# An FNet block with a GEGLU feed-forward: the DFT stage's side work laid out by a planner in the kernel

## The chip, the cores and the metric

One core of a Trainium2 chip. The metric is the device time of one execution in microseconds: the median of several runs of the kernel.

## What is computed

x has 2048 rows (the sequence) of 448 features, in f32. The weights of the two DFTs are given as matrices.

```python
a = einsum("bsd,ed->bse", ln(x), dft_hid_re)       # the hidden DFT, real and imaginary part
b = einsum("bsd,ed->bse", ln(x), dft_hid_im)
h = x + einsum("ts,bse->bte", dft_seq_re, a) - einsum("ts,bse->bte", dft_seq_im, b)
g = einsum("bsd,df->bsf", ln(h), w_gate)           # df = 1792
u = einsum("bsd,df->bsf", ln(h), w_up)
out = h + einsum("bsf,fd->bsd", gelu(g) * u, w_down)
```

ln is a layer norm without weights, gelu the tanh form.

## The kernel before, in words

Every f32 operand is split into two f16 halves, a high one (ACT rounds, `hi_part`, L105) and a low one (DVE subtracts the high half from the source, `lo_part`, L109 and L111), and each product is three matmuls: high by high, high by low, low by high. TensorE (PE) has by far the most work; ACT and DVE make its operands.

**The hidden DFT.** 16 tiles of 128 rows of x are normalised, split, turned by DMA transposes and multiplied (`feature_mm`, L422): a "feature tile", 22 matmuls of 448 columns, slot `F` in the code. `feature_out` takes the result out of PSUM. Half of the tiles (units 0 to 3) are split at once. The others (units 4 to 7) are kept in f32 in `b32`, a tile of the pool `ring` with tag "w" and two buffers; POOL (GpSimd) forms Strassen sums of them (`feature_sums`, L460 to L462) and `feature_split` splits these.

**The sequence DFT.** The 2048 x 2048 matrices are used in 8 passes `p` (256 rows of the result each, in four PSUM banks `acc`) of 8 units `u` (256 of the 2048 inputs). A unit's weights are loaded as f32 (`wr`, 512 KB, four buffers, L475). For a plain unit (0 to 3) they are split into `ws`, and PE does 24 matmuls of 448 columns (L518). For a Strassen unit (4 to 7) DVE first forms four sums (`wsum`, L480 to L482, two buffers); seven blocks are split into `ws` (three buffers), and PE does 42 matmuls of 224 columns. At the end of a pass `seq_out` adds the banks into `hx`, the residual stream, which is stored; its moments are taken, and for the first four passes (tokens of quarters 0 and 1) it is normalised, summed, split and transposed into `hops`, the moving operand of the gate and up products.

**The side work.** Gate and up weights come as 14 sets of f32 (`gu_raw`). Each needs four sums (L581 to L587, DVE) and four splits in pieces of 4, 2, 4 and 4 blocks, which gives a tile of 896 KB that is stored to `w_dram` (L626) and read back once per quarter (`gw`, L845). Ten sets are made during the DFTs, in a tile `gu_w` that also lies in `ring`, tag "w": one finished set can stand where `b32` wants to go. Sets 0, 1 and 2 come last and stay in SBUF for the first quarter. The other four sets (4, 7, 10, 13) are made in the first quarter in six "beats" each.

**The order.** PE's slots are a list: feature tiles, with units of pass 0 between them, then passes 1 to 7. Everything else is given to the slot numbers by hand: `plan(n, rank, what)` puts an action into slot `n`, and the slots are then written out in turn, sorted by rank. Each engine runs its own instructions in the order written and waits where an operand isn't there.

**The gate and up products.** 56 steps `t`, four quarters of 14. A step has 39 matmuls of 256 columns (L970) in seven products: `x_open` 6, `z_open` 6, `y_open` 6, `x_close` 5, `y_mid` 6, `y_close` 5, `z_close` 5. Between them ACT copies a bank (pY, L1009), takes u2 and u3 out of the bank Y (L1014, L1028) and does the gelu (g1, L1023; c12, L1047); DVE makes the hidden values hh. In the first quarter the down weights are prepared beside it by `down_prep`, a set for two steps: POOL makes sums `wd_s` (L215 to L218), ACT and DVE split the raw part (`down_hi(n, 0)`, `down_lo(n, 0)`) and the sums (`down_hi(n, 1)`, `down_lo(n, 1)`). From step 14 on the down products (L913) run between the gate and up products.

Of the kernel before, what the change touches and what calls it, by code (L numbers as in the profile page):

```python
# [32 lines left out]
def kernel(  # L33
# [262 lines left out]
    S_UNITS, WR = (4, 5, 6, 7), 3  # L296
# [142 lines left out]
    def feature_out(i):  # L439
        ps = feat.pop(i)  # L440
        if not is_s(i // 2):
            t = bop[i] = dft.tile([P, 2, 4, HD], F16, name=f"b{i}")
            for r in range(2):
                src, sc = ps[r][:, :D], (SC_AB, -SC_AB)[r]
                hi_part(t[:, 0, 2 * r : 2 * r + 2].rearrange("p o d -> p (o d)"), src, sc)
                lo_part(
                    t[:, 1, 2 * r : 2 * r + 2].rearrange("p o d -> p (o d)"),
                    src,
                    t[:, 0, 2 * r : 2 * r + 2].rearrange("p o d -> p (o d)"),
                    sc,  # L450
                )
            return
        b = b32[i] = ring.tile([P, 8, HD], F32, tag="w", bufs=2, name=f"b32_{i}")
        for r in range(2):
            hi_part(b[:, 2 * r : 2 * r + 2].rearrange("p o d -> p (o d)"), ps[r][:, :D], (SC_AB, -SC_AB)[r])


# [6 lines left out]
    def feature_split(i):  # L464
        b = b32.pop(i)
        t = bop[i] = dft.tile([P, 2, 7, HD], F16, name=f"b{i}")
        hi_part(t[:, 0], b[:, 1:8])
        lo_part(t[:, 1], b[:, 1:8], t[:, 0])
# [15 lines left out]
    def seq_split(p, u):  # L484
        r = wr.pop((p, u))
        t = ws[p, u] = dft.tile([P, 2, 7, 2 * P], F16, tag="ws", bufs=3, name=f"ws{p}_{u}")
        parts = [(slice(0, 1), r[:, 0:1]), (slice(1, 3), r[:, 2:4]), (slice(3, 7), wsum.pop((p, u)))] if is_s(u) else [(slice(0, 4), r)]
        for dst, src in parts:
            hi_part(t[:, 0, dst], src, D_SC)
        for dst, src in parts:  # L490
            lo_part(t[:, 1, dst], src, t[:, 0, dst], D_SC)

# [15 lines left out]
    def seq_mm(p, u, first, last):  # L508
# [4 lines left out]
        for cc in range(2):  # L513
# [7 lines left out]
            if is_s(u):  # L521
                for a, o, k, half in PRODUCTS:
                    for m, (lb, lw) in enumerate(TERMS):
                        mm(k, slice(half * HD, half * HD + HD), w[:, lw, a, cc * P : (cc + 1) * P], b[:, lb, o], end and m == 2)
            else:
                for k, a0 in ((0, 0), (1, 1)):
                    for r in range(2):
                        for m, (lb, lw) in enumerate(TERMS):
                            rhs = b[:, lb, 2 * r : 2 * r + 2].rearrange("p o d -> p (o d)")
                            mm(k, slice(0, D), w[:, lw, a0 + 2 * r, cc * P : (cc + 1) * P], rhs, end and r == 1 and m == 2)  # L530
# [12 lines left out]

    def seq_out(p):
        (X, Y, Z, W), _ = acc.pop(p)
        h = hp[divmod(p, 2)]
        e = e_of[p] = fops.tile([P, 4, HD], F32, tag="tt", name=f"e{p}")
        stt = V.scalar_tensor_tensor
        A.activation(e[:, 1], Z[:, 0:HD], AF.Copy, scale=SC_Y)
# [18 lines left out]
    class Weights:  # L568


        def __init__(self, f, pool, w_of):
            self.f, self.pool, self.w_of = f, pool, w_of
# [29 lines left out]

        def beat(self, k):

            if k < 2:
                self.sums(k == 0, k == 1)
            if k == 1:
                self.w = self.w_of()
            parts = self.parts(True) + self.parts(False)
# [6 lines left out]

        def split(self, of_raw):
            if of_raw:
                self.w = self.w_of()
            for s0, s1, src in self.parts(of_raw):  # L620
                hi_part(self.slots(0, s0, s1, src), src, W_SC)
            for s0, s1, src in self.parts(of_raw):
                lo_part(self.slots(1, s0, s1, src), src, self.slots(0, s0, s1, src), W_SC)
# [33 lines left out]

    for k, (i, i2) in enumerate(tiles_of):
# [728 lines left out]
```

## Time and profile before

| | before |
|---|---|
| median of 3 runs | 729.01 us (728.94 to 729.23) |
| the profiled execution | 729.15 us |
| its span | 727.4 us |
| PE busy | 708.2 us, 97% |
| DVE busy | 529.1 us, 73% |
| ACT busy | 396.1 us, 54% |
| POOL busy | 215.3 us, 30% |
| first gate/up matmul | at 361.58 us |

An engine's queue is run in order, so an instruction that waits holds all behind it. In a timeline row stand start, length, engine, line, operation, the tiles written and read, the shape and the count; the brackets give the idle time of the engine before it and what ended it. In a list of waits a row reads "engine tile line waited for engine tile line: us in total, times, the longest". In the table of windows each engine has its busy time and its count of instructions; granted clock, DMA share and GB/s stand at the end.

### The profile page before, as it was taken

The numbers are of one execution on the slowest core, as the hardware profiler recorded it, in microseconds if no ns is written. First come the engines' busy times: TensorE is split into PE (matmuls) and PEld (weight loads), VectorE is DVE, ScalarE is ACT, GpSimd is POOL, SyncE is SP. The second block draws the span as 40 slices with busy tenths as digits, with TensorE's granted clock in tenths as the row PEclk, the third lists the DMA queues.
The fourth block names the chain that finished last, engine by engine and source line by source line (L and its number), as shares of the span: only waits on it lengthen the run. The fifth ranks groups of instructions, "written<-read, shape, count | busy, mean of one in ns | idle before, by whom it ended". The sixth has DMA issues, their size and how long they took to land.

```text
span 727.4 us, 14930 instructions
## 1 busy us (share of the span) xinstructions
PE 708.2 (97%) x5944; PEld 574.1 (79%) x5944; DVE 529.1 (73%) x1054; ACT 396.1 (54%) x836; POOL 215.3 (30%) x241
## 2 busy tenths in 40 slices
PE   7999997989999999999998899999999999999998
PEld 5556555767777777686887789999999999999998
DVE  6777859698989998988478887576665756667520
ACT  5575646465757664645266665456555545555510
POOL 0023150000000000010025574465563756657230
PEclk9999999999999999999999999999999999999999
DMA  8464444656889697774268564957459486655401
GB/s 326 114 132 100 112 154 132 242 142 216 214 294 239 235 273 269 248 242 158 95 249 293 210 226 168 198 179 220 164 172 197 167 215 224 205 199 203 153 14 64
DMA packets 71765, 139.24 MB, mean 191 GB/s; under 512 B 41232, under 2 KB 47504, under 8 KB 71696
## 3 DMA queue, kind: packets, MB, share of 16 engines
q1 hardware_dynamic: 71696, 138.30, 60.8%
q8 instruction: 46, 0.75, 0.5%
q14 instruction: 23, 0.19, 0.1%
HBM read 108.79 MB, written 20.19 MB: 177 GB/s over the span
## 4 chain that ended last, share of the span: by engine, by line
PE 73%; DVE 13%; ACT 8%; issue 3%; DMA 2%; POOL 1%; SPq 0%; ACTq 0%; DVEq 0%
PE acc L518 29%; PE pY L970 13%; PE acc_d L913 11%; PE pX L970 8%; PE pZ L970 8%; DVE ws L111 2%; ACT ws L105 2%; ACT b L105 1%; DVE xs L109 1%; DVE st_x L328 1%; PE last_Z L1132 1%; PE last_X L1132 1%; PE last_Y L1132 1%; DVE b L109 1%; ACT x L355 1%
## 5 line engine op out<-in xcount | busy, mean ns | idle before, releaser
L518 PE MATMUL acc<-b,ws 128*128 128x224 f16 (+1 forms) x2112 | 277.4, 293 | 6.0 <-DVE ws L111 5.4
L518 PEld LDWEIGHTS <-ws 128*128 128x128 f16 x2112 | 202.8, 98 | 80.2 <-DVE ws L111 9.5
L970 PEld LDWEIGHTS <-gw 128*128 128x128 f16 x2067 | 201.9, 98 | 27.8 <-issue 7.3
L970 PE MATMUL pY<-hops,gw 128*128 128x256 f16 x901 | 122.5, 273 | 5.1 <-ACT pY L1009 5.1
L913 PE MATMUL acc_d<-wd,dn_w 128*128 128x224 f16 x882 | 105.1, 259 | 0.0
L111 DVE SCALAR_TENSOR_TENSOR ws<-wr,ws 128x256 f16<-128x256 f32 (+2 forms) x96 | 73.4, 790 | 19.3 <-ACT ws L105 18.7
L913 PEld LDWEIGHTS <-dn_w 128*128 128x128 f16 x882 | 85.0, 98 | 2.8
L105 ACT ACTIVATE ws<-wr 128x256 f16<-128x256 f32 (+2 forms) x96 | 63.0, 690 | 39.9 <-PE acc L518 21.5
L970 PE MATMUL pZ<-hops,gw 128*128 128x256 f16 x583 | 81.0, 273 | 0.8 <-DVE hh L980 0.7
L970 PE MATMUL pX<-hops,gw 128*128 128x256 f16 x583 | 79.2, 273 | 0.0
L1049 POOL TENSOR_TENSOR hh<-hh,c 128x256 f32<-128x256 f32 x42 | 32.1, 764 | 146.1 <-ACT c L1047 146.1
L215 POOL TENSOR_TENSOR wd_s<-wd 128x448 f32<-128x448 f32 x7 | 8.8, 1254 | 215.9 <-DVE wsum L480 199.3
L422 PEld LDWEIGHTS <-xT 128*128 128x128 f16 x352 | 34.2, 98 | 32.3 <-issue 1.2
L109 DVE TENSOR_TENSOR dn_w<-hh,dn_w 128x256 f16<-128x256 f32 x42 | 19.6, 467 | 53.1 <-ACT dn_w L105 53.1
L1063 POOL TENSOR_TENSOR dn_s<-hh 128x256 f32<-128x256 f32 x42 | 52.8, 1258 | 0.0
L105 ACT ACTIVATE ws<-wsum 128x1024 f16<-128x1024 f32 x32 | 33.6, 1050 | 35.1 <-DVE wsum L482 35.0
L109 DVE TENSOR_TENSOR dn_w<-dn_s,dn_w 128x640 f16<-128x640 f32 x42 | 46.3, 1103 | 6.2 <-ACT dn_w L105 4.4
L1014 ACT ACTIVATE u<-pY 128x256 f32<-128x256 f32 x56 | 21.5, 383 | 52.2 <-PE pY L970 52.1
L1009 ACT ACTIVATE pY<-pX 128x256 f32<-128x256 f32 x56 | 20.7, 369 | 49.1 <-PE pX L970 49.1
L422 PE MATMUL ab<-wh_hi,xT 128*128 128x448 f16 x224 | 45.5, 352 | 0.3 <-DVE b L111 0.2
L111 DVE SCALAR_TENSOR_TENSOR ws<-wsum,ws 128x1024 f16<-128x1024 f32 x32 | 39.1, 1222 | 2.6 <-ACT ws L105 2.6
L1062 POOL TENSOR_TENSOR dn_s<-hh 128x256 f32<-128x256 f32 x42 | 38.5, 916 | 0.0
(137 smaller groups left out, 937.0 us busy)
## 6 DMA issues: line engine op xcount, KB each, us to landing
gw<-w_dram SPq DMA_DIRECT2D x49, 896.0 KB, 4.8
wr<-in_w_seq_dram SPq DMA_DIRECT2D x64, 512.0 KB, 4.4
gu_raw<-in_w_gu_dram SPq DMA_DIRECT2D x28, 384.0 KB, 4.9
w_dram<-gu_w SPq DMA_DIRECT2D x10, 896.0 KB, 6.8
wd<-in_w_down_dram SPq DMA_DIRECT2D x14, 448.0 KB, 4.9
hx<-in_x_dram SPq DMA_DIRECT2D x8, 448.0 KB, 6.6
h_dram<-hx SPq DMA_DIRECT2D x8, 448.0 KB, 5.7
w_dram<-gw SPq DMA_DIRECT2D x4, 896.0 KB, 5.9
```

Source lines behind the costliest of these rows:

```text
L105: A.activation(dst, src, AF.Copy, scale=scale)
L109: V.tensor_sub(dst, src, hi)
L111: V.scalar_tensor_tensor(dst, src, scale, hi, op0=ALU.mult, op1=ALU.subtract)
L422: PE.matmul(feat[i][r][:, :D], xT[i][:, kx, :], w[:, kw, r * D : (r + 1) * D], start=n == 0, stop=n == 10,)
L518: PE.matmul(banks[k][:, cols], lhs, rhs, start=k not in begun, stop=stop, skip_group_check=True)
L913: PE.matmul(acc[k // 2][:, k % 2 * HD : (k % 2 + 1) * HD], a_of(la, a), b_of(lb, b), start=first and m == 0 and k % 2 == 0, stop=last and ...
L970: PE.matmul(ps, w[:, wl, wa + ws, :], ops[:, m + ms, :], start=first and n == 0, stop=last and n == len(terms) - 1, skip_group_check=True,)
L1014: A.activation(self.u2, self.Y, AF.Copy, scale=SC)
L1049: G.tensor_mul(c22, c22, self.c12)
L1062: G.tensor_add(s[:, 0:2], t[:, 0:2], t[:, 2:4])
L1063: G.tensor_sub(s[:, 2:4], t[:, 1:4:2], t[:, 0:4:2])
L1132: PE.matmul(banks[0][:, c * HD : (c + 1) * HD] if one else banks[c][:, 0:HD], last["h"][:, lh, f, tok], w, start=f == 0 and m == 0 and c = ...
```

## The change

1. **The planner.** All actions of the DFT stage from slot 3 on become `Task`s with an engine, a duration, a due time and the tasks that they follow (`lag` is a latency after these). Slots of PE are tasks too, with the lengths 4.16, 4.54 and 4.02 us. `arranged()` runs a clock in steps of 0.05 us; a free engine takes, of the tasks that are ready, the one that is due first. The instructions are written out in the order found. The order is fixed when the kernel is built. PE's order of slots stays.
2. **Buffers.** `wr` has three buffers instead of four. `ws` has four buffers of four blocks each; the four blocks of a Strassen unit's sums go to `wss` with two buffers. `wsum` has one buffer instead of two. The splits keep their pieces, and high and low halves become tasks of their own.
3. **Weights of the gate and up products.** Sets are made in the order 0 to 12. Each piece goes to a buffer `stage` (two of them) and is stored from there by a DMA of its own (256 KB, or 128 KB for the piece of two blocks): four stores for one. `gu_w` no longer lies in `ring`. Sets 0 to 3 are read back for the first quarter (before, set 3 alone was).
4. **The first quarter.** `down_hi(n, 1)` for n = 0 to 5 moves from the end of step 2n + 1 into step 2n + 2, behind `y_mid` and the beat.

```diff
-    S_UNITS, WR = (4, 5, 6, 7), 3
+    S_UNITS, WR_BUFS, WS_BUFS, WSS_BUFS, STAGE_BUFS = (4, 5, 6, 7), 3, 4, 2, 2
...
-        wr[p, u] = dft.tile([P, 4, 2 * P], F32, tag="wr", bufs=4, name=f"wr{p}_{u}")
+        wr[p, u] = dft.tile([P, 4, 2 * P], F32, tag="wr", bufs=WR_BUFS, name=f"wr{p}_{u}")
...
-        s = wsum[p, u] = dft.tile([P, 4, 2 * P], F32, tag="wsum", bufs=2, name=f"wsum{p}_{u}")
+        s = wsum[p, u] = dft.tile([P, 4, 2 * P], F32, tag="wsum", bufs=1, name=f"wsum{p}_{u}")
...
-        t = ws[p, u] = dft.tile([P, 2, 7, 2 * P], F16, tag="ws", bufs=3, name=f"ws{p}_{u}")
...
+    def seq_high(p, u):
+        ws[p, u] = [dft.tile([P, 2, 4, 2 * P], F16, tag="ws", bufs=WS_BUFS, name=f"ws{p}_{u}")]
+        for t, dst, src in seq_parts(p, u):
             hi_part(t[:, 0, dst], src, D_SC)
...
+    def seq_high_s(p, u):
+        t = dft.tile([P, 2, 4, 2 * P], F16, tag="wss", bufs=WSS_BUFS, name=f"wss{p}_{u}")
+        ws[p, u].append(t)
+        hi_part(t[:, 0], wsum[p, u], D_SC)
...
+        def high(self, k):
+            self.stage[k] = p2.tile([P, 2, 4, P], F16, tag="stage", bufs=STAGE_BUFS, name=f"gu_p{self.f}_{k}")
+            src, t = self.piece(k)
+            hi_part(t[0], src, W_SC)
+
+        def low(self, k):
+            src, t = self.piece(k)
+            lo_part(t[1], src, t[0], W_SC)
+            s0, s1, _ = (self.parts(True) + self.parts(False))[k]
+            rows = w_dram[self.f].rearrange("p (l o d) -> p l o d", l=2, o=14)
+            nc.sync.dma_start(rows[:, :, s0:s1], self.stage[k][:, :, 0 : s1 - s0])
...
+    class Task:
+        def __init__(self, engine, cost, due, what, after=(), begin=0.0, lag=0.1):
...
+    COST = {"F": 4.16, "P": 4.54, "S": 4.02}
...
+            load = add("SP", 0.1, T[n] - 12.0, lambda p=p, u=u: seq_load(p, u), after=done_with[g - WR_BUFS], lag=5.5)
...
+        low = add("V", 1.14 * size, T[n] - 0.4, lambda p=p, u=u: seq_low(p, u), after=[high])
...
-    order = list(reversed(in_dft[2:])) + in_dft[:2]
+    order = in_dft
...
+    def arranged():
+
+        now, left, busy, begun, n = 0.0, list(tasks), {"V": 5.6, "A": 4.7, "G": 0.0, "N": 0.0}, [], FIRST
...
+                able = [t for t in left if t.engine == engine and ready(t)]
+                if able:
+                    t = min(able, key=lambda t: t.due)
+                    cost = t.cost * (1.6 if engine == "V" and busy["G"] > now else 1.0)
...
+    gw_load(2)
     gw_load(3)
...
             down_hi(n, 0)
             down_lo(n, 0)
-            if n < NC - 1:
-                down_hi(n, 1)
...
             cur.y_mid()
             late_prep(2 * t)
+            if t > 0 and t % 2 == 0 and t < 2 * NC:
+                down_hi(t // 2 - 1, 1)
             nxt.z_open()
```

**ACT in the first quarter, before.** Step 3 of the gate and up products (numbers after u, g, pY and c12 are steps; wd is the down weights' split form, wd32_1 and wd_s_1 its raw and summed sources for set 1, gw7 a beat's piece):

```order
L1028 ACTIVATE u3_3_4482<-pY_3_4406 128x256
L1014 ACTIVATE u2_4_4501<-pY_4_4472 128x256
L105 ACTIVATE wd_4235<-wd32_1_4223 128x448
L105 ACTIVATE wd_4235<-wd_s_1_4452 128x1120
L105 ACTIVATE gw7_4521<-gu_raw7_4387 128x512
L1023 ACTIVATE g1_4_4530<-pX_4_4465 128x256
L1009 ACTIVATE pY_5_4539<-pX_5_4532 128x256
```

The same place in the changed kernel:

```order
L1173 ACTIVATE u3_3_4580<-pY_3_4503 128x256
L1159 ACTIVATE u2_4_4599<-pY_4_4570 128x256
L105 ACTIVATE wd_4333<-wd32_1_4321 128x448
L105 ACTIVATE gw7_4618<-gu_raw7_4484 128x512
L1168 ACTIVATE g1_4_4627<-pX_4_4563 128x256
L1154 ACTIVATE pY_5_4636<-pX_5_4629 128x256
L1192 ACTIVATE c12_3_4612<-c12_3_4612 128x256
L1173 ACTIVATE u3_4_4646<-pY_4_4570 128x256
L105 ACTIVATE gw7_4618<-gu_raw7_4484 128x256
L105 ACTIVATE wd_4333<-wd_s_1_4550 128x1120
L1159 ACTIVATE u2_5_4665<-pY_5_4636 128x256
```

The instruction that reads wd_s_1 stood ahead of g1 and of the copy pY; it now stands behind both, after u3 of the step.

**ACT near 90 us of the profile, before.** Feature tiles 14 and 15 (b32_14, b32_15 in the ring "w") and the end of a set of gate/up weights (gu_w12, in the same ring); ws0_6 and ws0_3 are weights of units 6 and 3 of pass 0:

```order
L105 ACTIVATE ws0_6_1022<-wsum0_6_988 128x1024
L105 ACTIVATE gu_w12_992<-gu_s12_948 128x512 x2
L105 ACTIVATE b32_14_1062<-ab14_0_1038 128x448
L105 ACTIVATE b32_14_1062<-ab14_1_1039 128x448
L105 ACTIVATE b32_15_1093<-ab15_0_1069 128x448
L105 ACTIVATE b32_15_1093<-ab15_1_1070 128x448
L105 ACTIVATE b14_1096<-b32_14_1062 128x1568
L105 ACTIVATE ws0_3_1144<-wr0_3_552 128x1024
```

The same feature tiles in the changed kernel (gu_p1_1 is piece 1 of set 1, in a stage buffer; wss0_7 the sums of unit 7 of pass 0):

```order
L105 ACTIVATE gu_p1_1_1084<-gu_raw1_921 128x256
L105 ACTIVATE b32_14_1114<-ab14_0_1052 128x448
L105 ACTIVATE b32_14_1114<-ab14_1_1053 128x448
L105 ACTIVATE ws0_7_1126<-wr0_7_1050 128x256
L105 ACTIVATE ws0_7_1126<-wr0_7_1050 128x512
L105 ACTIVATE wss0_7_1134<-wsum0_7_1122 128x1024
L105 ACTIVATE b32_15_1179<-ab15_0_1090 128x448
L105 ACTIVATE b32_15_1179<-ab15_1_1091 128x448
L105 ACTIVATE b14_1182<-b32_14_1114 128x1568
L105 ACTIVATE gu_p1_2_1195<-gu_s1_1047 128x512
```

The weights of unit 7 now come between the two feature tiles, ahead of the split of tile 14, and no tile of gate/up weights lies in the ring of b32.

More of the change, by code (lines that the diff above doesn't have):

```diff
@@ L656, in plan @@
         at(todo, n, *((rank, w) for w in what))
+    class Task:
+        def __init__(self, engine, cost, due, what, after=(), begin=0.0, lag=0.1):
+            self.engine, self.cost, self.due, self.what = engine, cost, due, what
+            self.after, self.begin, self.lag = [t for t in after if t], begin, lag
+            self.end = None
+    FIRST = 3
+    COST = {"F": 4.16, "P": 4.54, "S": 4.02}
+    spans = [COST["F" if s[0] == "F" else "S" if is_s(s[2]) else "P"] for s in slots]
+    T = {n: sum(spans[FIRST:n]) - sum(spans[n:FIRST]) for n in range(len(slots) + 1)}
@@ new lines, with add, fixed @@
+    tasks, steps = [], {}
+    def add(*args, **kw):
+        tasks.append(Task(*args, **kw))
+        return tasks[-1]
+    for n in range(FIRST, len(slots)):
+        steps[n] = Task("PE", spans[n], T[n], None)
+    def fixed(n, rank, engine, cost, what, after=(), lag=0.0):
+        if n < FIRST:
+            plan(n, rank, what)
+            return None
+        return add(engine, cost, T[n + 1], what, after=after, begin=T[n] - 1.0, lag=lag)
+    turned, out_of, bop_of, ring_w = {}, {}, {}, []
```

299 lines of the change are left out of this document (188 added, 111 removed).

## The prediction

> **What bounds the kernel now.** I read the page first: whichever engine is busy nearly all the time sets the end, and the question is then where it is held up.
>
> ```profile
> span 727.4 us, 14930 instructions
> PE 708.2 (97%) x5944; PEld 574.1 (79%) x5944; DVE 529.1 (73%) x1054; ACT 396.1 (54%) x836; POOL 215.3 (30%) x241
> ```
>
> PE has work for 97% of the span, so a change that leaves PE's instructions as they are (this one does: 11,890 rows in its queue before and after) can only win back time in which PE stands still or starts late. Second view: PE's timeline. A row there is a run of like matmuls: its start, its length, its count and the idle time before it.
>
> ```profile
> 28.71 4.70 PE L518 MATMUL acc<-b,ws 128*128 128x448 f16 x24
> 33.25 2.81 PE L422 MATMUL ab<-wh_hi,xT 128*128 128x448 f16 x14
> ...
> 46.63 2.81 PE L422 MATMUL ab<-wh_hi,xT 128*128 128x448 f16 x14
> ...
> 50.79 2.81 PE L422 MATMUL ab<-wh_hi,xT 128*128 128x448 f16 x14
> ...
> 63.28 4.19 PE L518 MATMUL acc<-b,ws 128*128 128x224 f16 x42
> 67.30 2.81 PE L422 MATMUL ab<-wh_hi,xT 128*128 128x448 f16 x14
> ...
> 111.85 1.06 PE L518 MATMUL acc<-b,ws 128*128 128x224 f16 x6 [1.31 <-DVE ws L111]
> ...
> 118.08 1.06 PE L518 MATMUL acc<-b,ws 128*128 128x224 f16 x6 [0.88 <-DVE ws L111]
> ...
> 147.64 4.39 PE L518 MATMUL acc<-b,ws 128*128 128x224 f16 x42 [0.89 <-DVE ws L111]
> 152.71 209.04 PE L518 MATMUL acc<-b,ws 128*128 128x224 f16 x1618 [0.67 <-DVE ws L111]
> 361.58 0.82 PE L970 MATMUL pX<-hops,gu_w 128*128 128x256 f16 x6
> ```
>
> From start to start an undisturbed plain unit of the sequence DFT takes 33.25 - 28.71 = 4.54 us, a feature tile 50.79 - 46.63 = 4.16, a Strassen unit 67.30 - 63.28 = 4.02. From 28.71 on the code has 32 plain units, 32 Strassen units and 12 feature tiles left: 145.3 + 128.6 + 49.9 = 323.8 us. It takes 361.58 - 28.71 = 332.9. So **9.1 us** are lost in the DFTs, and the rows say where: half a microsecond near 38 us, the rest in gaps before matmuls that wait for DVE's low halves of the weights, between 110 and 153 us. After 152.71 PE runs 209 us without one.
>
> The first quarter of the gate and up products, read the same way:
>
> ```profile
> 363.55 1.36 PE L970 MATMUL pX<-hops,gu_w 128*128 128x256 f16 x11
> ...
> 376.50 1.36 PE L970 MATMUL pX<-hops,gw 128*128 128x256 f16 x11
> ...
> 380.76 1.36 PE L970 MATMUL pX<-hops,gw 128*128 128x256 f16 x11
> ...
> 384.65 1.36 PE L970 MATMUL pY<-hops,gw 128*128 128x256 f16 x11 [1.22 <-ACT pY L1009]
> ...
> 394.32 1.36 PE L970 MATMUL pY<-hops,gw 128*128 128x256 f16 x11 [1.00 <-ACT pY L1009]
> ...
> 400.31 0.71 PE L970 MATMUL pZ<-hops,gw 128*128 128x256 f16 x5 [0.37 <-DVE hh L980]
> ...
> 429.75 0.71 PE L970 MATMUL pX<-hops,gw 128*128 128x256 f16 x5
> ```
>
> A step without a gap is 380.76 - 376.50 = 4.26 us. The 14 steps from 363.55 to 429.75 take 66.2 instead of 59.6: **6.6 us** lost, nearly all in five waits for ACT's copy pY, some 9.7 us apart, which is every second step. Behind it PE's timeline has no gap of half a microsecond, so these two places are all that the change can reach: 15.7 us.
>
> **The five waits for pY.** The list of waits names the partner, and ACT's timeline shows the queue:
>
> ```profile
> ACT wd L105 <- POOL wd_s L218: 9.0, 5, 2.0
> PE pY L970 <- ACT pY L1009: 5.1, 5, 1.2
> ```
>
> ```profile
> 380.15 0.57 ACT L105 ACTIVATE wd<-wd 128x448 f16<-128x448 f32 x1
> 382.40 1.14 ACT L105 ACTIVATE wd<-wd_s 128x1120 f16<-128x1120 f32 x1 [1.68 <-POOL wd_s L218]
> 383.44 0.61 ACT L105 ACTIVATE gw<-gu_raw 128x512 f16<-128x512 f32 x1
> 383.96 0.36 ACT L1023 ACTIVATE g<-pX 128x256 f32<-128x256 f32 x1
> 384.23 0.37 ACT L1009 ACTIVATE pY<-pX 128x256 f32<-128x256 f32 x1
> ```
>
> The high half of the down weights' sums (wd from wd_s, 1.14 us) stands in ACT's queue before POOL has made the sums; ACT waits 1.68 us, and behind it the copy at 384.23 comes too late for PE. It happens five times on both sides, so it is one cause. The change puts this instruction into the next step, behind u3 (the order rows show it). In these rows u3 would follow x_close, x_open and y_mid, 5 + 6 + 6 of the step's 39 matmuls, which PE begins at 380.76: it can't end before 383.0 (17 x 0.109 and its own 0.38), and POOL was done by 382.40. I count ACT's wait as gone. Its 1.14 us now stand ahead of u2, for which PE's twelve matmuls of z_open and y_open (1.3 us) are cover; if that cover goes, u2 is late by up to 1.1 us, but the bank that it reads is written again only 21 matmuls (2.3 us) after. What is next late is DVE, which has the same work in 1.2 us less for every two steps. I leave 0.8 us in this stage, two gaps like the one behind DVE's hh at 400.31: gain 5.8, between 2.9 (half of it) and 6.6.
>
> **The gaps between 110 and 153 us.** What happens before them:
>
> ```profile
> 95.23 0.98 ACT L105 ACTIVATE b<-ab 128x448 f32<-128x448 f32 x2 [7.50 <-DMA w_dram<-gu_w]
> ```
>
> ```profile
> 97.64 2.17 DVE L109 TENSOR_TENSOR b<-b,b 128x1568 f16<-128x1568 f32 x1 [8.69 <-ACT b L105]
> ```
>
> The f32 features of the Strassen tiles and the finished gate/up weights share a ring of two buffers; ACT can't put down the features of tile 14 until a store of weights has landed, POOL and DVE stand behind it, and the work of four feature tiles, two Strassen units and a set of weights comes in a heap after 97 us. The change ends the sharing (weights go to a stage buffer of their own), so this wait of 7.5 us has no cause left, and PE's gaps lose their source. What would be late next is the amount of DVE's work:
>
> ```profile
> 60.00:100.00 40.00, 40.00 (x255) 24.59 (x253) 25.91 (x49) 20.72 (x34) 13.52 (x12) 1.00 0.42 110
> 100.00:150.00 50.00, 44.69 (x327) 30.39 (x325) 42.99 (x67) 28.02 (x47) 7.57 (x7) 1.00 0.53 177
> 150.00:200.00 50.00, 49.31 (x374) 35.66 (x372) 46.59 (x94) 33.28 (x66) 0.00 (x0) 1.00 0.72 197
> 200.00:250.00 50.00, 50.00 (x388) 37.22 (x386) 45.93 (x99) 33.49 (x63) 0.00 (x0) 1.00 0.84 262
> ```
>
> ```profile
> 79.74 0.55 DVE L581 TENSOR_TENSOR gu_s<-gu_raw 128x384 f32<-128x384 f32 x1
> ...
> 81.47 1.15 DVE L111 SCALAR_TENSOR_TENSOR b<-ab,b 128x448 f16<-128x448 f32 x2
> ...
> 84.66 1.02 DVE L111 SCALAR_TENSOR_TENSOR gu_w<-gu_raw,gu_w 128x512 f16<-128x512 f32 x2
> 85.59 1.02 DVE L111 SCALAR_TENSOR_TENSOR ws<-wr,ws 128x256 f16<-128x256 f32 x2
> ...
> 87.67 1.29 DVE L111 SCALAR_TENSOR_TENSOR gu_w<-gu_s,gu_w 128x512 f16<-128x512 f32 x2
> ```
>
> DVE's column is the third pair. A set of gate/up weights costs it (81.47 - 79.74) + (85.59 - 84.66) + 1.29 = 3.9 us. Before, two of the ten sets are done by 150 us; in the new order three, and the sums of a fourth (1.7 us), stand ahead of the same unit: 5.6 us more. From 60 to 150 us DVE was busy 68.9 of 90 us; with 5.6 more, and some 8 us of PE's gaps taken out, it must do 74.5 in 82, or 91%. The two windows behind show 92 to 93% with PE hardly waiting, so it fits, if the new order keeps DVE's waits small. After 150 us DVE has 5.6 us less to do than before. Nothing else is added for the engines: both orders hold the same DVE, ACT and POOL work (10 more DVE rows are the same operations, no longer merged). Bounds of what is left of the 9.1: nothing, as after 152.71, or all of it. I take 1.8, not quite three gaps of the 0.67 us seen last, since the order is fixed ahead with one landing time for all loads, and the landings vary. Gain 7.3.
>
> **What is paid.** The loads of f32 sequence weights (wr) get three buffers instead of four, and each weight store becomes four.
>
> ```profile
> DMA to landing us min/median/max: 3.5/4.4/9.3
> ```
>
> ```profile
> w_dram<-gu_w SPq DMA_DIRECT2D x10, 896.0 KB, 6.8
> ```
>
> Thirty more stores and three more loads of 896 KB (gate/up weights 0 to 2 are read back) pass SP's queue in some 330 us; SP issues in order, so a wr load stands behind a piece whose low half DVE hasn't written, for at most one such piece, 0.7 us. I cost this at nothing as long as a wr load is asked for a full turn of the ring ahead: three units, 12.8 us, against a landing of 4.4. The read-backs 2 and 3 are asked for before the last units end and are first used two steps into the products, so their landing is covered too.
>
> The Trainium skill speaks against this part: "DMA: Bandwidth & Descriptors", in the section on measured bandwidth, says to batch DMAs to 1 MiB or more, and its section on the anatomy of one DMA gives about 2.0 us fixed for each. As an estimate from that page, four pieces would take 10.1 us of transfer for 4.1 in one, so 60 us more over ten sets. No run here shows a piece; if it took hold it would do so as in the second rival.
>
> **Sum.** 729.15 us is the profiled execution's own time (1.75 outside its span, and 0.14 above the median of 729.01). 729.15 - 7.3 - 5.8 = 716.05, and I forecast 716.0. All 15.7 gained would be 713.4.
>
> **Rivals.** *DVE becomes the bound.* For: 91% is needed where 43.0 of 50 us was reached between 100 and 150. If DVE stays idle for the same 7.0 us there, the stretch shrinks only by what goes ahead of it into the idle time from 60 to 100, about a set of weights: 3.9 won instead of 7.3, so 729.15 - 3.9 - 5.8 = 719.5, and 722.3 with the first quarter at its lower bound. Against: the idle time had the named cause. Chance 0.14.
>
> *The ring of three wr buffers runs dry.* This one ends slower. A buffer's turn is the landing plus DVE's and ACT's work on it plus the wait for its place in their queues; each microsecond over 12.8 costs a third of one per unit, on 60 units. It decides from a loss of 14.9 us, 0.25 per unit, a turn of 13.6. With landings of 7 us, between the median and the longest row, and 7 us in the queues, the turn is 14.0, the loss 24, and the time 729.15 - 5.8 - 9.1 + 24 = 738. For: the queues' DMA share is 0.84 from 200 to 250 us, and the pieces and read-backs come on top. Against: at the median landing the queues may take 8.4 us. Chance 0.07.
> The Trainium skill's batching rule (the page named above) would come in here, as longer landings.
>
> *The wait in the first quarter only moves.* POOL's sums are later still, or ACT's 1.14 us ahead of u2 holds PE: half of the 5.8 stays, 719. Chance 0.09.
>
> **How the numbers follow.** My forecast has 0.70, and 713.4 to 718.5 as its own range. The first and third rival end between 718.5 and 722.3. Together these hold nine in ten; the range 713.4 to 722 leaves out the slower rival and the tails. A difference of 0.2% (1.5 us) is what a measurement of this kernel can tell from none. Slower: 0.07; the same 0.02, where losses cancel; faster 0.91.
>
> **What would show it.** Right: on PE's timeline no row with an idle note between 100 and 153 us, the first pX near 354 instead of 361.58, steps of 4.26 us after it, the row at 429.75 near 416.7; among the waits no ACT wd behind POOL over a few tenths, and no ACT b behind a store. Wrong: PE waits for ws by DVE between 130 and 250 with DVE over 95% busy (first rival); ACT's or DVE's first reading of wr waits for its load (second); PE pY still behind ACT (third).

## The result, and the profile after

| | before | after |
|---|---|---|
| median | 729.1 us (728.94 to 729.23, 4 runs) | 720.89 us (718.33 to 721.34, 4 runs) |
| ratio to before, with its 95% interval | | 0.988 [0.9857, 0.9903] |
| the profiled execution | 729.15 us | 720.96 us |
| its span | 727.4 us | 719.2 us |
| first gate/up matmul | 361.58 us | 357.25 us |

The change gains 8.2 us. The prediction was 716.0, a gain of 13.1, with a range of 713.4 to 722.0. The runs of the change also lie further apart than those of the kernel before: 3.0 us against 0.3. Among the experiments below, one profiled execution (the fifth) took 2694 us where the other four of that kernel took 716.16 to 719.36; the four alone are counted.

PE's timeline after, at the two places where the kernel before lost time (start, length, engine, line, operation, tiles, shape, count, and in brackets the idle time before it):

```profile
28.98 4.70 PE L533 MATMUL acc<-b,ws 128*128 128x448 f16 x24
...
240.62 4.91 PE L533 MATMUL acc<-b,ws 128*128 128x448 f16 x28 [1.19 <-DVE ws L111]
...
250.85 0.27 PE L533 MATMUL acc<-b,wss 128*128 128x224 f16 x1 [1.11 <-DVE wss L111]
...
357.25 0.82 PE L1115 MATMUL pX<-hops,gw 128*128 128x256 f16 x6
359.21 1.36 PE L1115 MATMUL pX<-hops,gw 128*128 128x256 f16 x11
...
380.79 0.70 PE L1115 MATMUL pZ<-hops,gw 128*128 128x256 f16 x5 [0.49 <-DVE hh L1125]
...
406.02 0.81 PE L1115 MATMUL pZ<-hops,gw 128*128 128x256 f16 x6 [1.09 <-DVE c L1125]
...
421.32 0.71 PE L1115 MATMUL pX<-hops,gw 128*128 128x256 f16 x5
```

Read as in the prediction: the DFTs take 357.25 - 28.98 = 328.3 us where 323.8 are needed, so 4.5 are lost instead of 9.1. The 14 steps of the first quarter take 421.32 - 359.21 = 62.1 where 59.6 are needed, so 2.5 are lost instead of 6.6. That is 4.6 and 4.1 gained, 8.7 together; 0.3 of it goes because the first unit starts at 28.98 instead of 28.71, and a few tenths are spread over the rest.

Between 100 and 225 us PE has no idle row at all, as announced. But there is a new loss where the kernel before had none: of the 4.5 us, 0.8 lie between 55 and 60 us, nearly all of the rest between 230 and 273 us, most of it in the rows at 240.62 and 250.85. DVE is late there. The windows say whether it had too much to do (DVE's busy time is the third pair):

```profile
100.00:150.00 50.00, 50.00 (x390) 37.49 (x389) 48.77 (x82) 30.87 (x55) 7.48 (x6) 1.00 0.60 188
...
200.00:250.00 50.00, 48.45 (x382) 36.42 (x380) 42.18 (x89) 31.16 (x57) 0.00 (x0) 1.00 0.81 231
```

It had not. From 100 to 150 us DVE is busy 48.77 of 50 us and PE waits for nothing; from 200 to 250 it is busy only 42.18, and PE stands. So DVE is idle for some other reason, and the list of waits names it (engine, tile, line, what it waited for: us in total, times, the longest):

```profile
ACT ws L105 <- DMA wr<-in_w_seq_dram: 34.1, 12, 6.9
...
DVE wsum L480 <- DMA wr<-in_w_seq_dram: 16.7, 6, 4.6
```

Before, neither row existed. ACT and DVE now stand before loads of sequence weights that haven't landed. The view of the tile wr says that the loads themselves are not much slower, since the median was 4.4 us and the longest 9.3 before:

```profile
DMA to landing us min/median/max: 3.5/4.7/9.2
```

So they start too late. SP's own list of waits shows what it stands before, here the stores of pieces (L637):

```profile
SPq L637 <- DVE gu_p L111: 56.7, 18, 5.7
```

SP's timeline shows the order of its queue, in a stretch 25 and 35 us ahead of PE's two gaps:

```profile
207.45 0.52 SPq L637 DMA_DIRECT2D w_dram<-gu_p  x1
208.44 6.98 SPq L289 DMA_TRANSPOSE hops<-xs  x4
215.51 0.55 SPq L637 DMA_DIRECT2D w_dram<-gu_p  x1
216.11 1.10 SPq L475 DMA_DIRECT2D wr<-in_w_seq_dram  x2
217.30 0.52 SPq L637 DMA_DIRECT2D w_dram<-gu_p  x1
217.87 1.27 SPq L475 DMA_DIRECT2D wr<-in_w_seq_dram  x1
```

Two suspects come out of this. SP stands 56.7 us before pieces (`gu_p`, in the stage buffers) whose low half DVE has not written, up to 5.7 us at a time. And at 208.44 four DMA transposes of the finished residual rows (L289) follow one another and hold SP for 7 us; behind them three wr loads, which should have started one by one, leave within 2 us of each other. (Blocks of 7.05 and 7.44 us stand at 146.74 and 176.53 too, and PE has no gap behind these; the runs don't say why the third was the one that cost time.) DVE's timeline shows the effect: its sums of the next unit wait 4.60 us.

```profile
221.04 0.69 DVE L480 TENSOR_TENSOR wsum<-wr 128x512 f32<-128x512 f32 x1 [4.60 <-DMA wr<-in_w_seq_dram]
```

SP's timeline of the kernel before has these transposes in two pairs, with a wr load between them:

```profile
219.88 3.44 SPq L289 DMA_TRANSPOSE hops<-xs  x2
223.73 0.33 SPq L475 DMA_DIRECT2D wr<-in_w_seq_dram  x1
224.11 4.44 SPq L289 DMA_TRANSPOSE hops<-xs  x2
```

Three theories for the 3.5 us or so lost after 200 us follow: the ring of three wr buffers asks too late; SP's queue holds the loads up (behind unwritten pieces, or behind the block of transposes); or DVE's amount of work, against which the windows already speak. The transfers of the many small pieces are a fourth.

### The profile page after: what moved, and what is told of

Read it like the earlier page. It is cut to its first block, busy times and chain, and to the rows that moved or that the text cites. A ratio compares the mean times of both kernels' runs of the same rounds, so it can differ in the third digit from the quotient of the medians.

```text
span 719.2 us, 15074 instructions
## 1 busy us (share of the span) xinstructions
PE 705.9 (98%) x5944; PEld 573.8 (80%) x5944; DVE 534.0 (74%) x1054; ACT 396.1 (55%) x836; POOL 215.3 (30%) x241
## 4 chain that ended last, share of the span: by engine, by line
PE 68%; DVE 17%; DMA 5%; ACT 4%; issue 4%; SPq 2%; DVEq 0%; ACTq 0%
PE acc L533 20%; PE pY L1115 12%; PE acc_d L1060 11%; PE pZ L1115 8%; PE pX L1115 8%; PE ab L422 5%; DMA wr<-in_w_seq_dram 3%; DVE ws L111 2%; DVE xs L109 2%; DMA gu_raw<-in_w_gu_dram 1%; DVE wsum L480 1%; PE last_Z L1277 1%; PE last_X L1277 1%; PE last_Y L1277 1%; DVE wss L111 1%
## 5 line engine op out<-in xcount | busy, mean ns | idle before, releaser
L1115 PEld LDWEIGHTS <-gw 128*128 128x128 f16 x2184 | 213.4, 98 | 25.5 <-issue 3.5
L533 PE MATMUL acc<-b,ws 128*128 128x448 f16 (+1 forms) x1344 | 222.2, 312 | 1.2 <-DVE ws L111 1.2
L533 PEld LDWEIGHTS <-ws 128*128 128x128 f16 x1344 | 130.4, 98 | 72.5 <-DVE ws L111 2.3
L1115 PE MATMUL pY<-hops,gw 128*128 128x256 f16 x952 | 129.1, 273 | 0.0
L533 PE MATMUL acc<-b,wss 128*128 128x224 f16 x768 | 95.0, 259 | 1.3 <-DVE wss L111 1.1
L1115 PE MATMUL pZ<-hops,gw 128*128 128x256 f16 x616 | 85.5, 272 | 2.3 <-DVE c L1125 1.1
L105 ACT ACTIVATE ws<-wr 128x256 f16<-128x256 f32 (+2 forms) x96 | 62.6, 689 | 41.0 <-DMA wr<-in_w_seq_dram 34.1
L1115 PE MATMUL pX<-hops,gw 128*128 128x256 f16 x616 | 83.2, 273 | 0.0
L111 DVE SCALAR_TENSOR_TENSOR ws<-wr,ws 128x256 f16<-128x256 f32 (+2 forms) x96 | 73.8, 794 | 9.3 <-ACT ws L105 8.9
L533 PEld LDWEIGHTS <-wss 128*128 128x128 f16 x768 | 73.9, 98 | 2.1 <-DVE wss L111 2.1
L1208 POOL TENSOR_TENSOR dn_s<-hh 128x256 f32<-128x256 f32 x42 | 52.4, 1248 | 0.0
L105 ACT ACTIVATE wss<-wsum 128x1024 f16<-128x1024 f32 x32 | 33.6, 1051 | 32.0 <-DVE wsum L482 27.2
```

What stands on the lines that cost most here:

```text
L105: A.activation(dst, src, AF.Copy, scale=scale)
L111: V.scalar_tensor_tensor(dst, src, scale, hi, op0=ALU.mult, op1=ALU.subtract)
L533: PE.matmul(banks[k][:, cols], lhs, rhs, start=k not in begun, stop=stop, skip_group_check=True)
L1115: PE.matmul(ps, w[:, wl, wa + ws, :], ops[:, m + ms, :], start=first and n == 0, stop=last and n == len(terms) - 1, skip_group_check=True,)
L1208: G.tensor_sub(s[:, 2:4], t[:, 1:4:2], t[:, 0:4:2])
```

## The experiments

Each experiment ran beside the kernel before, on one of three chips. In the table, the losses are worked out from PE's timeline of each profiled execution as above (first row of acc to first pX, less 323.8; from the first to the last of the rows of the 14 steps, less 59.6).

| kernel | median, us | ratio, 95% interval | DFTs lose | first quarter loses |
|---|---|---|---|---|
| before | 729.1 | | 9.1 | 6.6 |
| the change | 720.89 | 0.9857 to 0.9903 | 4.5 | 2.5 |
| 1 ring of four | 717.73 | 0.9829 to 0.9856 | 1.9 | 2.8 |
| 2 stores placed later | 725.54 | 0.9936 to 0.9961 | 9.5 | 1.9 |
| 3 wd at its old place | 724.51 | 0.9918 to 0.9943 | 4.2 | 5.9 |
| 4 wd's move on before | 725.28 | 0.9935 to 0.9963 | 8.9 | 2.6 |
| 5 transposes spread | 717.1 | 0.9815 to 0.9852 | | |
| 6 early set earlier, on before | 723.32 | 0.9901 to 0.9929 | 4.3 | 5.8 |
| 7 stores later, four stages | 722.45 | 0.9889 to 0.9918 | 5.8 | 2.6 |
| 8 ring of four, set 13 in the DFTs | 716.50 | 0.9808 to 0.9833 | 1.9 | 1.1 |
| 9 transposes spread, again | 717.82 | 0.9825 to 0.985 | 2.2 | 2.9 |
| 10 the change, again | 721.04 | 0.9855 to 0.9894 | 4.7 | 3.3 |
| 11 both edits on before | 720.30 | 0.9856 to 0.9885 | 4.6 | 2.6 |
| 12 the eighth, with two more edits | 716.82 | 0.9813 to 0.9842 | 1.9 | 3.7 |

The fifth has no trace that can be used; the ninth is the same kernel, run again for its trace. Where an edit changes buffers or tasks (1, 2, 7, 8 and 12), the planner also finds another order of DVE's, ACT's and SP's rows; in the ninth, DVE, ACT, POOL and PE keep theirs.

**1. Ring of four.**

```diff
-    S_UNITS, WR_BUFS, WS_BUFS, WSS_BUFS, STAGE_BUFS = (4, 5, 6, 7), 3, 4, 2, 2
+    S_UNITS, WR_BUFS, WS_BUFS, WSS_BUFS, STAGE_BUFS = (4, 5, 6, 7), 4, 4, 2, 2
```

> The change with four wr buffers instead of three, and nothing else set by hand (the planner then asks for each load one unit earlier). Theory of the ring (three buffers are asked for too late, so loads land after ACT and DVE want them): ACT's 34.1 us and DVE's 16.7 us of waits for wr fall to under a third, the loss in the DFTs from 4.5 to about 2 us, so 718.4 us. Theory of the queue (a load stands on SP behind a piece whose low half is not written): a load asked for earlier stands in the same queue, but has a unit more to spare; the waits fall by about half, and the time to 719.5. Theory of DVE's amount of work: no change, 720.5 to 721.5.

717.73 us (717.31 to 718.30, four runs). PE has no idle row between 60 us and the first pX, and the waits for wr nearly vanish. From the view of the tile wr, who waited for it and how long:

```profile
who waited for it (us, times):
  ACT wss L105: 12.4, 7
  DVE ws L111: 9.3, 8
  ACT ws L105: 4.3, 3
  DVE wsum L480: 1.8, 1
```

ACT's reading of wr waited 34.1 us in the change, now 4.3 (only 0.6 of it for a load, by the list of waits); DVE's sums waited 16.7, now 1.8. DVE's amount of work is therefore not the cause. Nor are the pieces' transfers: all 40 stores are still there and the DFTs lose 1.9 us, 1.6 of which lie in one place at 55 us. But the result alone doesn't tell the ring from the queue, since a load asked for a unit earlier also survives a longer hold-up on SP, where a block of four transposes still takes 7.58 us in this run.

**2. Stores placed later.** The store leaves `low` and becomes a task of SP's own.

```diff
-            stages.append(add("N", 0.0, 0.0, lambda: None, after=[low], lag=7.0))
+            wait = add("N", 0.0, 0.0, lambda: None, after=[low], lag=3.0)
+            put = add("SP", 0.1, due(0.4 + 0.2 * m), lambda f=f, m=m: gu[f].put(m), after=[wait])
+            stages.append(add("N", 0.0, 0.0, lambda: None, after=[put], lag=5.0))
```

> The change with each piece's store put into SP's order 3 us behind the planned end of its low half, instead of at its start; ring of three, same instructions. Theory of the queue: SP's 56.7 us of waiting for DVE's gu_p go to under 15 us, the loads behind the pieces start on time, the waits for wr fall by more than half, and the DFTs lose about 2.5 us instead of 4.5: 719 us. Theory of the ring: the queue is not what delays the loads; waits for wr and time stay within 1 us of the change, 720 to 722. Theory that pieces land slowly (many small transfers): no change either, since the transfers are the same.

725.54 us: 4.7 slower than the change, which no theory expected. SP's wait for the pieces did fall, from 56.7 to 15.1 us, but a stage buffer is now given back later, and ACT stands before the next piece, by the list of waits of this run:

```profile
ACT gu_p L105 <- DMA w_dram<-gu_p: 43.5, 11, 12.2
```

The longest of these waits on ACT's timeline:

```profile
226.42 0.63 ACT L105 ACTIVATE gu_p<-gu_s 128x512 f16<-128x512 f32 x1 [12.24 <-DMA w_dram<-gu_p]
```

In the change these waits were 7.3 us in all. Behind the waiting ACT stand the high halves of ws, and 10 us later PE waits 2.42 us for ws, its longest single wait in this run. The experiment thus exchanged one hold-up for another and settled nothing about the queue; the seventh takes the new one away.

**3. The down weights' high half back at its old place**, in the changed kernel.

```diff
             down_lo(n, 0)
+            if n < NC - 1:
+                down_hi(n, 1)
...
-            if t > 0 and t % 2 == 0 and t < 2 * NC:
-                down_hi(t // 2 - 1, 1)
```

> The change with the second part of the down weights' high half back at its old place. Theory (this one move makes all the gain in the first quarter, 4.1 us by the trace): five waits of ACT wd behind POOL come back, PE waits for ACT's pY again, 725 us. Rival (the gaps in the first quarter went because DVE and ACT arrive there in another state): 721 to 722.

724.51 us, and the two old rows are back in the list of waits:

```profile
ACT wd L105 <- POOL wd_s L218: 8.2, 5, 1.9
PE pY L1117 <- ACT pY L1156: 4.3, 5, 1.2
```

The DFTs lose 4.2 us as in the change, the first quarter 5.9 instead of 2.5. So this one move makes nearly all of the gain there.

**4. The same move alone, on the kernel before** (the diff of the third, the other way).

> The kernel before with that one move alone. Theory: 4.1 to 5.8 us less than before, 723.3 to 725, and the DFTs keep their gaps between 110 and 153 us. Rival: within 1 us of 729.

725.28 us, 3.9 less than the 729.16 of the kernel before beside it. The first quarter loses 2.6, the DFTs 8.9 with all their old gaps. Third and fourth agree: the move is worth 3.6 to 3.9 us.

**5 and 9. The transposes spread.** Nothing moves but these four instructions in SP's order; the rows of PE, DVE, ACT and POOL stay the same in the same order.

```diff
             for k in range(4):
-                add("SP", 0.1, t0 + 28.0 + k, lambda q=q, j=j, k=k: ffn_transpose(q, j, (k,)), after=[t])
+                wait = add("N", 0.0, 0.0, lambda: None, after=[t], lag=5.0 * k)
+                add("SP", 0.1, t0 + 28.0 + k, lambda q=q, j=j, k=k: ffn_transpose(q, j, (k,)), after=[wait])
```

> The change (ring of three) with the four transposes of each finished pair of rows put 5 us apart in SP's order, as the kernel before had them in two pairs apart, instead of one behind the other; the order of PE, DVE, ACT and POOL stays row for row the same. Theory of the queue: the 7 us in which SP does nothing but these four transposes (208.44 to 215.42) made the three wr loads behind them start in a bunch at 216 to 218; PE's two gaps at 240.6 and 250.9 (2.6 of the 4.5 us lost in the DFTs) go, 718.3 us. Theory of the ring: three buffers are asked for too late whatever SP's order is; 720 to 721.5.

> The kernel of the fifth experiment once more, for its trace and beside the change on one chip: the four transposes 5 us apart in SP's order and nothing else. Theory of the queue: 717.1 us again (the median of its four runs), two to four us below the change; no PE gap over 1 us at 240 to 251, wr loads no longer start in a bunch behind a 7 us block, ACT's and DVE's waits for wr under half of 34.1 and 16.7 us. Theory that the first timing was luck (the change itself ranged from 718.3 to 721.3): 719 to 721 and the two gaps in the trace.

717.1 us, and again 717.82 (716.99 to 718.97), beside 721.04 for the change on the same chip; the two intervals (0.9825 to 0.985, and 0.9855 to 0.9894) do not overlap. SP's timeline of the ninth, at the place shown above:

```profile
207.86 1.30 SPq L289 DMA_TRANSPOSE hops<-xs  x1
210.15 0.53 SPq L637 DMA_DIRECT2D w_dram<-gu_p  x1
210.73 2.02 SPq L475 DMA_DIRECT2D wr<-in_w_seq_dram  x2
212.80 1.25 SPq L289 DMA_TRANSPOSE hops<-xs  x1
215.89 0.53 SPq L637 DMA_DIRECT2D w_dram<-gu_p  x1
216.48 0.59 SPq L475 DMA_DIRECT2D wr<-in_w_seq_dram  x1
217.12 1.23 SPq L289 DMA_TRANSPOSE hops<-xs  x1
```

Two of the three wr loads start at 210.73 instead of 216.11. PE's two gaps at 240 and 251 are gone; in all of the DFTs after 60 us one idle row is left:

```profile
265.31 4.91 PE L533 MATMUL acc<-b,ws 128*128 128x448 f16 x28 [0.70 <-DVE ws L111]
```

The DFTs lose 2.2 us, with three wr buffers. ACT's waits for wr came down to 17.9 us and DVE's only to 14.8, not under half as expected: what is left of them is mostly covered. So the block of transposes in SP's queue is what started the loss, and the ring of three is what let it through. The fourth buffer alone removes all of it; the spreading alone removes it but for about 1 us, near 265 and 270.

**6. The early set of weights 12.7 us earlier, on the kernel before.** The ring stays shared.

```diff
-    early_f = [s + 4 for s in pairs[1:3]]
+    early_f = [pairs[1] + 1, pairs[2] + 4]
```

> The kernel before with the first of its two early sets of gate/up weights three slots (12.7 us) earlier, so that its store has landed before the features of tile 15 ask for its buffer in the shared ring; the ring stays shared and DVE has the same work before 150 us. Theory (the shared ring makes the gaps between 110 and 153 us): ACT's 7.50 us wait behind the store goes, DVE's 8.69 us with it, and most of the 8.6 us of PE's gaps: 722 us. Rival (DVE simply has too much to do in that stretch): the gaps stay, 728 to 729.5.

723.32 us. ACT no longer waits for a store of gu_w; DVE still waits 4.47 us for ACT's b, where it had waited 8.69. Of PE's gaps between 110 and 153 us the first half is gone, and the second half, 2.6 us between 141 and 148 us, stays. PE's timeline of this run, its rows with an idle note between 95 and 250 us:

```profile
141.22 0.59 PE L518 MATMUL acc<-b,ws 128*128 128x224 f16 x3 [0.18 <-DVE ws L111]
142.70 4.39 PE L518 MATMUL acc<-b,ws 128*128 128x224 f16 x42 [0.90 <-DVE ws L111]
147.76 102.97 PE L518 MATMUL acc<-b,ws 128*128 128x224 f16 x792 [0.67 <-DVE ws L111]
```

The DFTs lose 4.3 instead of 9.1. What makes the second half of the gaps no run shows; DVE's amount of work, the rival, is not excluded for it. One edited line undoes as much of the old loss in the DFTs as the whole planner did.

**7. Stores placed later, with four stage buffers.**

```diff
-    S_UNITS, WR_BUFS, WS_BUFS, WSS_BUFS, STAGE_BUFS = (4, 5, 6, 7), 3, 4, 2, 2
+    S_UNITS, WR_BUFS, WS_BUFS, WSS_BUFS, STAGE_BUFS = (4, 5, 6, 7), 3, 4, 2, 4
```

> The stores placed later, as in the second experiment, with four stage buffers instead of two; ring of three wr buffers. Theory (that run lost 4.7 us because a late store gives its stage buffer back late, and ACT stands before it): ACT's 43.5 us of waits for stores fall under 5 us and the time to 718 to 719.5, below the change's, since SP no longer stands before unwritten pieces. Rival (what costs is loads behind the transposes, and the stores' place is beside the point): 720 to 721.5. Rival (more pieces in flight make the loads land later): 724 or more.

722.45 us. ACT's wait for the stores is gone, which confirms the reading of the second. But the time does not fall below the change's (0.9889 to 0.9918 against 0.9857 to 0.9903), a miss for the theory that the pieces hold up the loads. By SP's list of waits the standing moved: 8.5 us before the stores instead of 56.7, but 71.2 instead of 36.0 at the wr loads behind DVE's last reading of their buffer (`SPq L475 <- DVE ws L111`), and 25.6 before loads of gu_raw behind unwritten pieces. And at 211.90 the four transposes again take 5.91 us in one block, and PE has the change's two gaps in the same size, besides a new one of 0.79 us at 214.76.

```profile
242.19 4.91 PE L533 MATMUL acc<-b,ws 128*128 128x448 f16 x28 [1.19 <-DVE ws L111]
...
252.42 0.27 PE L533 MATMUL acc<-b,wss 128*128 128x224 f16 x1 [1.11 <-DVE wss L111]
```

**8. Ring of four, and set 13 made in the DFTs.**

```diff
-    LATE = {4: 0, 7: 6, 10: 12, 13: 18}
+    LATE = {4: 0, 7: 6, 10: 12}
...
-        ahead = {1: 5, 2: 6, 4: 8, 5: 9, 7: 11, 8: 12, 10: 14, 12: 15, 13: 16}.get(t) if t <= NF else t + 2
+        ahead = {1: 5, 2: 6, 4: 8, 5: 9, 7: 11, 8: 12, 9: 13, 10: 14, 12: 15, 13: 16}.get(t) if t <= NF else t + 2
```

> The change with four wr buffers, and with one of the four sets of gate/up weights that are made during the first quarter (number 13) made in the DFTs instead, stored and read back as the others. Theory (the gaps left in the first quarter, 0.65, 0.62 and 1.25 us before pZ, come from the amount of DVE's work on these sets, and DVE has room in the DFTs after 300 us): the 1.25 us gap near 403 us goes, perhaps the one near 391, no new one in the DFTs: 716.2 us against 717.7. Rival (the eleventh set takes DVE's lead away in the DFTs): 717.5 to 720.

716.50 us (716.23 to 716.62), the lowest median of all and below both kernels; its interval just overlaps that of the first experiment. The first quarter loses 1.1 us; the gap that was at 406.02 in the change is gone, and the DFTs carry the eleventh set without a new gap. What made that gap, in the change, is on DVE's timeline:

```profile
403.71 0.59 DVE L599 TENSOR_TENSOR gu_s<-gu_raw 128x384 f32<-128x384 f32 x1 [2.10 <-DMA gu_raw<-in_w_gu_dram]
...
405.23 0.41 DVE L1184 SCALAR_TENSOR_TENSOR hh<-pY,g 128x256 f32<-128x256 f32 x1
405.56 0.41 DVE L1125 SCALAR_TENSOR_TENSOR c<-pZ,u 128x256 f32<-128x256 f32 x1
```

Set 13's sums stand in DVE's queue before their load has landed, 2.10 us, and hh and c behind them come too late for PE, which waits 1.09 us for c. So the expectation was right about the gap, but not about its reason: by this row it is a wait for a load, and not an amount of work.

The same wait and the same gap stand in the fourth experiment, which has the move of the down weights and no planner (DVE's row, then PE's):

```profile
407.81 0.75 DVE L581 TENSOR_TENSOR gu_s<-gu_raw 128x384 f32<-128x384 f32 x1 [1.95 <-DMA gu_raw<-in_w_gu_dram]
```

```profile
410.28 0.82 PE L968 MATMUL pZ<-hops,gw 128*128 128x256 f16 x6 [1.10 <-DVE c L978]
```

The eleventh, also without a planner, has them too (1.94 and 1.09 us); the third, the planner with the move undone, has neither. So they came with the move. In the fourth SP issues set 13's load at 401.90, right behind DVE's last reading of set 10's gu_raw, which ends at 401.82. With the move DVE comes to set 13's sums 4.0 us after that reading (the fourth, the eleventh and the change), without it 5.4 us after (before and the third); the load has landed 5.9 to 6.0 us after it with the move, and 4.2 to 4.5 without. Why it lands later is open.

**10. The change again.**

> The change itself, unchanged, on the same chip as the runs beside it: 718 to 721.5 us as before, and if the length of a run hangs on how long the few loads behind SP's transposes take to land, with a wider spread than the runs beside it.

721.04 us, and six runs from 717.03 to 722.72. PE's two waits of 1.19 and 1.11 us in the DFTs are there again, at 240.15 and 250.39.

**11. Two edits on the kernel before, no planner** (the diffs of the fourth and the sixth together).

> The kernel before with two edits and no planner: the early set of weights 12.7 us earlier (the sixth experiment, 6.2 us) and the down weights' high half at its new place (the fourth, 3.9 us). If the two losses are separate, the gains add: 729.2 - 6.2 - 3.9 = 719.1 us, below the change. If one hid the other: 721 to 723.

720.30 us (the expectation was 719.1, below the change), a gain of 9.4 where the two alone gained 3.9 and 6.3 against the kernel before beside them. The losses are separate and add up but for 0.8 us. With these few edited lines the old scheme is as fast as the changed kernel (their intervals cover each other).

**12. The eighth, with the transposes spread and the first set's sums not before 25 us of the plan.**

```diff
-        s1 = add("V", 0.95, due(0.2), lambda f=f: gu[f].sums(True, False), after=[raw] + freed, begin=t0 - 20.0)
+        s1 = add("V", 0.95, due(0.2), lambda f=f: gu[f].sums(True, False), after=[raw] + freed, begin=max(t0 - 20.0, 25.0))
```

> The eighth experiment (ring of four, set 13 in the DFTs), with the transposes spread as in the fifth and the first set's sums not before 25 us of the plan, so that DVE has the low halves of the features first at 55 us. Theory: PE's gap of 1.6 us at 55 us goes or halves, the spreading adds nothing to a ring of four: 715.2 us against 716.5. Rival (the sums only move the gap to the next feature tile): 716 to 717.

716.82 us (716.19 to 719.00): the rival. The gap at 55 us stays, and with a ring of four the spread transposes add nothing that shows. The first set's sums did move, from 42.28 to 57.62, behind the features' low halves; but the planner put low halves of unit weights in front of these instead, from 50.09 to 52.2, and they start at 55.08 as before (55.11 in the eighth). So these sums alone do not cause the gap; whether DVE's amount of work there does is open. The profiled execution, 719.00, was the longest of the four, and PE's timeline shows where its 2.5 us over the eighth went:

```profile
390.36 0.81 PE L1116 MATMUL pZ<-hops,gw 128*128 128x256 f16 x6 [1.35 <-DVE c L1126]
...
393.54 0.71 PE L1116 MATMUL pZ<-hops,gw 128*128 128x256 f16 x5 [1.16 <-DVE hh L1126]
```

Just ahead DVE stands 2.64 us before gu_raw, for set 10 this time; the eighth has no such wait.

## Why the prediction held, and which step of it failed

**What bounds the kernel.** Right. PE's 9.1 and 6.6 us were all there was to win, and two separate causes made more than half of them: the fourth and the sixth experiment took them away one at a time, the eleventh together.

**The five waits for pY.** Right in the mechanism, as the third and fourth experiment show in both directions: ACT's wait behind POOL goes, and with it the wait for pY. The size was off: 5.8 us were forecast, 4.1 measured in the trace and 3.6 to 3.9 in the times. "What is next late is DVE" was right; 0.8 us for it was too little, since 2.5 are left. I had counted DVE's durations and not its loads. The largest piece of the rest is the gap at 406.02, behind DVE's wait for gu_raw; in the kernel before DVE waits for no load in this stage. That wait is a price of the move itself, since it stands in the fourth and eleventh experiment without a planner and not in the third: DVE gets to set 13's sums sooner, and the load that they need can't start before DVE has done with set 10's.

**The gaps between 110 and 153 us.** Right in the result for this stretch, and in the cause for half of it. The wait behind the store in the shared ring was the source of the first half of the gaps (sixth experiment); the second half stayed there, so its cause is open. In the changed kernel no gap is left between 100 and 225 us. DVE went through that stretch at 48.77 of 50 us, more than the 91% that I asked of it, and PE never waited. The term is 4.6 instead of 7.3 because some 3.5 us came back after 225 us.

**What is paid.** This is the step that failed: "I cost this at nothing as long as a wr load is asked for a full turn of the ring ahead". The list of what passes SP's queue named 30 stores and three loads and left out the four transposes per finished pair of rows, which the planner prices at 0.1 us of SP and so puts one behind the other. In the block at 208.44 they hold SP for 1.44, 2.86, 1.23 and 1.20 us, together 7, each starting within 0.1 us of the end of the one before. With a turn of 12.8 us and a landing of 4.7, 7 us on SP leave about 1 us for ACT's and DVE's queues, by this estimate. The ninth experiment, which moves these four instructions alone, wins 3.2 us, and its DFTs lose 2.2. That this is close to the 1.8 that I had left them is luck, since 0.8 of it lies near 55 us, where I had expected nothing. I also wrote that a load stands behind a piece "for at most one such piece, 0.7 us": SP stood up to 5.7 us there. But that wait was worth little: in the ninth SP still stands there 54.5 us, and the DFTs lose about 1 us after 60 us; in the first 59.7, and they lose nothing there. Moving the stores, in the second and seventh, gained nothing.

**The many small stores.** Costing them at nothing was right. The view of the DMA queues gives for the kernel before (packets, MB, share of 16 engines' span):

```profile
q1 hardware_dynamic: 71696, 138.30, 60.8%
```

The same view of the change has this line, and the pieces with their count, size and median landing:

```profile
q1 hardware_dynamic: 81568, 141.06, 63.4%
...
w_dram<-gu_p SPq DMA_DIRECT2D x30, 256.0 KB, 2.9
w_dram<-gu_p SPq DMA_DIRECT2D x10, 128.0 KB, 3.7
```

The engines were busy for 0.634 x 719.2 - 0.608 x 727.4 = 14 us more in all, three further read-backs among it. A piece lands in 2.9 or 3.7 us where a whole set took 6.8. Added up by these medians that is 30 x 2.9 + 10 x 3.7 = 124 us against 68; but landings overlap, and the first experiment has no PE gap in the DFTs after 60 us with all the pieces in place. The Trainium skill's rule to batch DMAs to 1 MiB or more ("DMA: Bandwidth & Descriptors", its section on measured bandwidth) thus did not decide anything here. The 60 us that I had estimated from that page of the Trainium skill are close to the 56 us by which the landings grew in sum, but four times the 14 us by which the queue was busier. The Trainium skill gives both the 2.0 us and the rule beside measurements of DMAs issued from GpSimd, which I had left out; these stores are issued by SP.

**The rivals.** DVE as the bound was wrong: PE waited where DVE was busy 42.18 of 50 us and not where it was busy 48.77. The ring of three running dry gave its sign, ACT and DVE waiting for wr, and cost some 3.5 us and not 24: a turn was too long behind a block of transposes, not at every unit. The rival in the first quarter was wrong: no wait for pY is left.

**The signs.** PE's clean stretch from 100 to 153 us, and the missing waits of ACT behind POOL and behind a store of gu_w, came as announced. The first pX came at 357.25 and not near 354, the row that was at 429.75 at 421.32 and not near 416.7. The forecast was 4.9 us too low: what I left in the two stages, 1.8 and 0.8 us, was too little by 2.7 and 1.7, and the start and the rest of the run took another half.

## What to carry to other kernels

Where a planner orders a queue, every entry needs its real time on the engine that issues it: four transposes at 0.1 us each in the plan were a block of 7 us on SP in the trace, and the loads behind them were late. Before a ring is made smaller, add up the longest stretch in which its queue does something else, the landing and the reader's own queue; three buffers had no room for a block that four took without a gap on PE. And look for the one wait that starts a chain before rebuilding the order: two edits of a few lines did to the old kernel what the planner did with its ring of three. With a ring of four the planner goes further (0.9829 to 0.9856 of the time before, against 0.9856 to 0.9885 for the two edits).

## What the runs showed of the hardware

A DMA transpose of the finished rows holds the queue that issues it for 1.18 to 2.92 us in the ninth experiment, with a median of 1.29, against a median of 0.38 us for the 512 KB loads. Transposes are short to write down and long to issue.

Ten runs of the change lie between 717.03 and 722.72 us, four of the ring of four between 717.31 and 718.30, and five of the eighth between 716.23 and 716.62; eleven of the kernel before, run beside the last four experiments, between 728.86 and 730.86. Loads of one size landed in 3.5 to 9.2 us in one execution of the change. That a kernel whose loads are asked for just in time passes this spread on to its time is likely, but no run shows it.
